# Row sums ordered by head, and two broadcast reads from DRAM where four stood, in a top-k attention and mixer kernel

## The chip, the core and the metric

The kernel runs on one core of one Trainium2 chip. The metric is the device time of one execution in microseconds (us); lower is better. A core has a matrix engine (PE, with its weight loads listed apart as PEld), a vector engine (DVE), an activation engine (ACT), a general engine (POOL), and a queue engine (SP) that here only issues transfers. Each engine takes its instructions strictly in the order of the program. Transfers (DMAs) are issued by SP and by ACT; on ACT an issue stands in the same order as its computing instructions.

## The reference

Attention over the 32 largest scores of each row, then a mixer with a low-rank token part and a two-layer channel part:

```python
# q, k, v: (8, 8, 576, 64)
scores = scale * np.matmul(q, k.transpose(0, 1, 3, 2))
kth = np.partition(scores, -32, axis=-1)[..., -32:-31]
scores = np.where(scores >= kth, scores, -1e9)
attn = np.exp(scores - np.max(scores, axis=-1, keepdims=True))
attn = attn / (np.sum(attn, axis=-1, keepdims=True) + 1e-09)
x = np.matmul(attn, v).transpose(0, 2, 1, 3).reshape(8, 576, 512)
# U: (576, 32), V: (32, 576), w_ch1: (512, 2048), w_ch2: (2048, 512)
u = x + (x.transpose(0, 2, 1) @ U @ V).transpose(0, 2, 1)
out = u + np.maximum(u @ w_ch1, 0.0) @ w_ch2
```

The division by the row sum is what the change touches: every row of `attn` has one sum, and the kernel multiplies by its inverse after the product with `v`.

## The kernel before, in words

The 64 heads are taken two at a time: 32 pairs `g`, four to a batch entry. The 576 rows of a head are four tiles of 128 (`t` 0 to 3) and a tail of 64 (`t` 4), in which the two heads of a pair share one tile. The program is one long hand-made order: a loop over steps, one tile each (the last tile of a pair and its tail share a step), and in each step a fixed sequence of calls for tiles in different stages. In the order in which a tile passes them:

- `scores` (L336, L381, L401): the score products on PE, copied to `Ssb` (the tail to `Stail`) by ACT.
- `fold`, `split` and `pair` (L432, L434, L435): each row is halved into its larger and smaller entries; POOL adds, DVE takes the maximum, POOL subtracts.
- `front` (L487, L485, L502, L515, L520): DVE finds the 32 largest of a row by rounds of "eight largest" and "replace them". ACT makes the negated row maximum (`nmax`, L506) and the threshold (`least`, L546), masks (L549; POOL subtracts in L550), and takes exponentials (L439), whose sums over the row go to one column of a small tile `den` each. `den` has nine columns: two heads by four tiles, and the tail.
- `blocks` and `back` (L576, L582, L591): DVE transposes the exponentials in blocks, four DMAs from SP put them into a DRAM tile `away`, and one DMA from ACT reads it back as `PT`. `back` runs one step after `blocks`.
- `values` (L688, L691, L700): the product with `v`, features on the partitions, copied to `XT` by ACT. It is not yet divided by the row sums.
- `inverse` (L629, L631, L635), for pairs 4 to 31: once a pair's nine sums are there, DVE inverts and transposes them to nine rows of 128, and four DMAs from SP write these to a DRAM tile `rd` of nine rows: row `2t+h` for tile `t` and head `h`, and row 8 for the tail, with 64 numbers for each head.
- `scale` (L641 to L651), two thirds of a step later: DMAs from ACT read `rd` into a tile of 128 by 576, `sc`, so that each of the 64 partitions of a head holds all inverse sums of that head.
- `mixed` (L719, L720, then L725 to L778): POOL multiplies `XT` by `sc` into `uT`; then comes the token part of the mixer. L777 uses the tile `sc` again as a scratch.
- `mlp` (L810, L823, L828, L839, L840): the channel part of an earlier batch entry. Its products are spread between the others by `fill()`; ACT applies the rectifier (`hT`, L823) and copies (`oT`, L839), POOL adds `uT` (L840).

For the first four pairs the sums are used in another layout (`den4`), without `rd` and `sc`. The attention of all pairs with the channel part of earlier entries between it lasts to about 1545 us; after it the channel part of the last entry runs alone (`closing`).

Two things set when a DMA can start. It stands in its engine's order. And in the built program every DMA of SP and ACT, in the order of the program, is given one of eight semaphores in turn; before it is issued, its engine waits until the last DMA with the same semaphore has landed, unless an earlier wait already made that sure. So a DMA can hold its engine back for the sake of a transfer that it has nothing else to do with.

Of the kernel before, what the change touches and what calls it, by code (L numbers as in the profile page):

```python
# [26 lines left out]
def kernel(  # L27
# [28 lines left out]
    nc = tc.nc  # L56
    B, H, S, D = q.shape
    P = 128
# [4 lines left out]
    NT, TAIL = 4, 64  # L63
    MAIN = NT * P
    HALF = S // 2
    assert S == MAIN + TAIL and D == 64 and H % 2 == 0 and C == 512 and TOPK % 8 == 0
    NPAIR = H // 2
# [69 lines left out]
    def half(h):  # L137
        return slice(h * D, (h + 1) * D)
# [298 lines left out]
    def weigh(chunk, E, nmax, total=None):  # L437

        nc.scalar.activation(E, chunk, AF.Exp, bias=nmax, scale=SCALE, accum_out=total)  # L439

    def ways(g, t):

        if (g, t) == (NPAIR - 1, NT - 1):
            return (0,), (), (1,)
        if (g, t) == (NPAIR - 1, NT):
            return (0,), (), ()
        if t == NT:
            return (), (), (0,)
        return ((), (1,), (0,)) if g < NPAIR else ((), (), (1, 0))
# [4 lines left out]
    def front(tiles):  # L454

        lanes = []
        for g, t in tiles:  # L460
            if t == 0:
                dens[g] = small.tile([P, 2 * NT + 1], F32, tag="den", name="den", bufs=3)
            S2, den = S2s.pop((g, t)), dens[g]
            early, pooled, gaps = ways(g, t)
            n = S2.shape[1]
            fold_of = folds.pop((g, t), None)
            for c in (1, 0) if n == 2 else (0,):
                slot = c if n == 2 or len(tiles) == 1 else 2
                lanes.append((
                    slot,  # L470
                    S2[:, c],
                    den[:, 2 * t + c : 2 * t + c + 1],
                    [a[:, c] for a in fold_of] if fold_of else None,
                    "early" if c in early else "pooled" if c in pooled else "gap" if c in gaps else "",
                ))
        W = len(lanes)
        first = small.tile([P, 3, 8], F32, tag="first", name="first", bufs=3)
        nmax = small.tile([P, 3], F32, tag="nmax", name="nmax", bufs=4)
        curs, places, ms = {}, {}, {}
        halves = [(lane[0], *lane[3]) for lane in lanes if lane[3]]  # L480
        for at_, step in ((0, 0), (0, 1), (8, 0)):
            for slot, upper, lower in halves:
                spot = upper[:, HALF + at_ : HALF + at_ + 8]
                if step:
                    nc.vector.match_replace(lower, spot, lower, NEG)  # L485
                else:
                    nc.vector.max(spot, lower)  # L487
        for slot, chunk, _, fold_of, _ in lanes:
            if fold_of:
                curs[slot] = fold_of[0]  # L490
            else:
                curs[slot] = chunk
                if slot == 2:
                    places[slot] = attn.tile([P, S], F32, tag="tplace", name="place", bufs=1)
                else:
                    places[slot] = attn.tile(
                        [P, 2, HALF + TOPK // 2], F32, tag="upper", name="upper"
                    ).rearrange("p c n -> p (c n)")[:, 0:S]
            ms[slot] = first[:, slot]
        order = [lane[0] for lane in lanes]  # L500
        for c in order:
            nc.vector.max(ms[c], curs[c])  # L502
        yield
        for i in range(1, TOPK // 8):
            if i == 1:
                nc.scalar.mul(nmax[:, 0:W], first[:, 0:W, 0], -SCALE)  # L506
                Es = {}
                for c, chunk, _, _, way in lanes:
                    if way == "early":
                        Es[c] = attn.tile([P, S], F32, tag="E", name="E")  # L510
                        weigh(chunk, Es[c], nmax[:, c : c + 1])
            for c in order:

                nxt = places.pop(c, curs[c])
                nc.vector.match_replace(nxt, ms[c], curs[c], NEG)  # L515
                curs[c] = nxt
            m8 = small.tile([P, 3, 8], F32, tag="m8", name="m8", bufs=4)
            for c in order:
                ms[c] = m8[:, c]
                nc.vector.max(ms[c], curs[c])  # L520
            yield
        for c, chunk, total, _, way in lanes:
            if way == "pooled":
                gap = attn.tile([P, S], F32, tag="E", name="E")
                nc.gpsimd.tensor_scalar(gap, chunk, ms[c][:, 7:8], NEG, ALU.is_lt, ALU.mult)
                nc.gpsimd.tensor_tensor(chunk, chunk, gap, ALU.add)  # L526
        for c, chunk, total, _, way in lanes:
            if way == "early":
                nc.vector.scalar_tensor_tensor(
                    out=chunk,  # L530
                    in0=chunk,
                    scalar=ms[c][:, 7:8],
                    in1=Es[c],
                    op0=ALU.is_ge,
                    op1=ALU.mult,
                    accum_out=total,
                )
        if t == NT:
            del qkTs[g]
        yield  # L540
        gaps = [lane for lane in lanes if lane[4] == "gap"]
        if gaps:
            slots = [lane[0] for lane in gaps]
            lo, hi = min(slots), max(slots) + 1
            least = small.tile([P, 3], F32, tag="least", name="least", bufs=3)
            nc.scalar.mul(least[:, lo:hi], m8[:, lo:hi, 7], WIDEN)  # L546
            for c, chunk, *_ in gaps:
                gap = attn.tile([P, S], F32, tag="E", name="E")
                nc.scalar.activation(gap, chunk, AF.Relu, bias=least[:, c : c + 1], scale=-WIDEN)  # L549
                nc.gpsimd.tensor_tensor(chunk, chunk, gap, ALU.subtract)  # L550
            yield
        rest = [lane for lane in lanes if lane[4] != "early"]
        if len(gaps) > 1:
            c, chunk, total, *_ = rest.pop(0)
            weigh(chunk, chunk, nmax[:, c : c + 1], total)
            yield
        for c, chunk, total, *_ in rest:
            weigh(chunk, chunk, nmax[:, c : c + 1], total)
        if t == NT and g != NPAIR - 1:
            nc.scalar.activation(den, den, AF.Identity, bias=eps)  # L560
        yield
# [77 lines left out]
    def scale(g):  # L639

        rd = scales.pop(g)  # L641
        sc = attn.tile([P, S], F32, tag="scale", name="scale", bufs=1)
        scales[g] = sc
        for h in range(2):
            nc.scalar.dma_start(
                sc[half(h), 0:MAIN].rearrange("p (t n) -> p t n", t=NT),
                rd[0 : 2 * NT].rearrange("(t h) n -> h t n", h=2)[h : h + 1].to_broadcast([D, NT, P]),
            )
            nc.scalar.dma_start(
                sc[half(h), MAIN:S], rd[2 * NT : 2 * NT + 1, half(h)].to_broadcast([D, TAIL])  # L650
            )  # L651

    def values(g, t):

# [521 lines left out]
    t = 0  # L1176
# [5 lines left out]
    for n in range(STEPS + 2):  # L1182
        if n < STEPS:
            g, t = steps[n][0]
            if t == 0 and g < NPAIR:
                load(g + 1)
            if t == (1 if g < NPAIR else 2) and g + 1 < NP:
                ready = prep(g + 1)
            fronts[n] = front(steps[n])
            next(fronts[n])  # L1190
        else:
            t = NT
# [93 lines left out]
        if n < STEPS and n - 2 >= ALONE and len(tiles(n - 2)) > 1:  # L1286
            scale(steps[n - 2][0][0])
# [3 lines left out]
        if n >= STEPS:  # L1291
            if n == STEPS:
                inverse(NP - 1, 0, 2 * NT + 1)
                scale(NP - 1)
            weighted(n - 2)
# [61 lines left out]
```

## Time and profile before

| what | value |
| --- | --- |
| time, median of three runs | 1684.32 us (1682.92 to 1688.65) |
| the profiled execution | 1686.09 us, of which 1684.0 us are its span |
| mean granted PE clock | 0.963 |
| DMA packets | 295631, 189.42 MB; queue of SP 259728 packets, queue of ACT 35744 |
| `scale` reads of ACT | 56 of 128 KB (L645) and 56 of 16 KB (L649), two of each per pair for 28 pairs |
| `rd` writes of SP (L635) | 112 of 1.1 KB, median issue 316 ns |
| `PT` reads of ACT (L591) | 104 of 576 KB, median issue 326 ns |
| L719, multiply by `sc` | 56 on POOL, median 738 ns; L720 28, median 330 ns |

The span runs from the first to the last instruction of the program; the profiled execution's own time is 2.1 us longer. Busy time counts an engine's computing instructions; an engine that waits before a DMA issue counts as idle, and such issues are listed with a "q" behind the engine's name (ACTq, SPq). A number in square brackets behind an instruction is the idle time just before it and what ended that.

### The profile page before, as it was taken

The numbers are of one execution on the slowest core, as the hardware profiler recorded it, in microseconds if no ns is written. First come the engines' busy times: TensorE is split into PE (matmuls) and PEld (weight loads), VectorE is DVE, ScalarE is ACT, GpSimd is POOL, SyncE is SP. The second block draws the span as 40 slices with busy tenths as digits, with TensorE's granted clock in tenths as the row PEclk, the third lists the DMA queues.
The fourth block names the chain that finished last, engine by engine and source line by source line (L and its number), as shares of the span: only waits on it lengthen the run. The fifth ranks groups of instructions, "written<-read, shape, count | busy, mean of one in ns | idle before, by whom it ended". The sixth has DMA issues, their size and how long they took to land.

```text
span 1684.0 us, 30301 instructions
## 1 busy us (share of the span) xinstructions
PE 1569.8 (93%) x9638; PEld 1189.6 (71%) x9638; DVE 1546.0 (92%) x4393; ACT 992.5 (59%) x2475; POOL 1000.3 (59%) x853
## 2 busy tenths in 40 slices
PE   4667798999899999999999999999999999999999
PEld 2444466777577886778777787778777787778776
DVE  7999998899999999999999999999999999995452
ACT  4888777665655656556655566556655566564320
POOL 4778668666656565655656565655656565653620
PEclk7787798999999999999999999999999999999999
DMA  3323232254555555555455555554555555543001
GB/s 87 96 74 96 61 94 73 56 128 130 136 128 131 134 151 131 127 138 131 124 128 139 127 139 135 132 139 124 133 128 132 133 140 136 132 126 109 10 1 29
DMA packets 295631, 189.42 MB, mean 112 GB/s; under 512 B 178768, under 2 KB 279984, under 8 KB 295472
## 3 DMA queue, kind: packets, MB, share of 16 engines
q1 hardware_dynamic: 259728, 117.62, 30.2%
q10 hardware_dynamic: 35744, 69.88, 13.6%
q8 instruction: 76, 1.25, 0.3%
q14 instruction: 83, 0.68, 0.1%
HBM read 116.49 MB, written 70.91 MB: 111 GB/s over the span
## 4 chain that ended last, share of the span: by engine, by line
DVE 47%; PE 33%; DMA 8%; SPq 4%; issue 3%; ACT 2%; POOL 1%; ACTq 0%; DVEq 0%; POOLq 0%
DVE m L520 13%; DVE upper L515 11%; PE mm L828 9%; PE mm L810 8%; DVE y L576 5%; DVE first L502 4%; DVE upper L487 4%; DMA ld<-in_k_dram 3%; PE sc L336 3%; DVE place L515 3%; PE mm L904 3%; DVE lower L485 3%; PE O L691 2%; DMA PT<-away 2%; PE sc L904 2%
## 5 line engine op out<-in xcount | busy, mean ns | idle before, releaser
L810 PE MATMUL mm<-uT,w 128*128 128x320 f32 (+1 forms) x1792 | 468.1, 413 | 14.5 <-ACT hT L823 14.1
L550 POOL TENSOR_TENSOR Ssb<-Ssb,E 128x576 f32<-128x576 f32 x243 | 340.0, 1419 | 208.8 <-ACT E L549 208.4
L828 PE MATMUL mm<-hT,w 128*128 128x320 f32 (+1 forms) x1792 | 462.8, 408 | 0.0
L810 PEld LDWEIGHTS mm<-uT,w 128*128 128x128 f32 x1792 | 336.1, 192 | 120.2 <-ACT hT L823 23.3
L828 PEld LDWEIGHTS mm<-hT,w 128*128 128x128 f32 x1792 | 332.5, 190 | 93.6 <-issue 11.0
L520 DVE MAX8 m<-upper 128x8 f32<-128x304 f32 (+1 forms) x780 | 377.8, 539 | 0.7
L515 DVE MATCH_REPLACE8 upper<-m,upper 128x304 f32<-128x304 f32 (+1 forms) x520 | 266.8, 534 | 0.0
L435 POOL TENSOR_TENSOR lower<-lower,upper 128x576 uint32<-128x576 uint32 x108 | 152.9, 1416 | 162.0 <-DVE upper L434 161.7
L439 ACT ACTIVATE Ssb<-Ssb,nmax 128x576 f32<-128x576 f32 x258 | 201.8, 783 | 32.9 <-POOL Ssb L526 9.9
L432 POOL TENSOR_TENSOR lower<-Ssb 128x576 uint32<-128x576 uint32 x108 | 152.4, 1411 | 93.3 <-ACT Ssb L381 48.7
L487 DVE MAX8 upper<-lower 128x8 f32<-128x288 f32 x432 | 176.8, 461 | 15.9 <-POOL lower L435 15.8
L336 PE MATMUL sc<-qkT 64*128 64x288 f32 (+1 forms) x1056 | 179.6, 462 | 11.0 <-ACT Ssb L390 7.8
L549 ACT ACTIVATE E<-Ssb,least 128x576 f32<-128x576 f32 x243 | 176.3, 769 | 4.2
L381 ACT COPY Ssb<-sc 128x576 f32<-128x576 f32 x216 | 127.8, 644 | 61.6 <-PE sc L336 61.6
L576 DVE STREAM_TRANSPOSE y<-Ssb 128x512 f32<-128x512 f32 (+1 forms) x312 | 157.7, 581 | 0.3 <-ACT Ssb L439 0.2
L823 ACT ACTIVATE hT<-mm 128x320 f32<-128x320 f32 (+1 forms) x224 | 91.3, 410 | 102.7 <-PE mm L810 97.9
L691 PE MATMUL O<-PT,va 128*64 128x128 f32 x2048 | 144.5, 285 | 0.0
L336 PEld LDWEIGHTS sc<-qkT 64*128 64x128 f32 (+1 forms) x1056 | 96.0, 197 | 52.0 <-issue 17.4
L691 PEld LDWEIGHTS O<-PT,va 128*64 128x64 f32 x2048 | 113.3, 140 | 16.4 <-issue 2.0
L515 DVE MATCH_REPLACE8 upper<-first,upper 128x304 f32<-128x304 f32 x216 | 100.4, 487 | 0.0
L485 DVE MATCH_REPLACE8 lower<-upper,lower 128x288 f32<-128x288 f32 x216 | 96.3, 465 | 0.0
L434 DVE TENSOR_TENSOR upper<-sc,Ssb 128x576 f32<-128x576 f32 x108 | 83.3, 772 | 11.5 <-ACT Stail L401 11.5
(264 smaller groups left out, 2246.9 us busy)
## 6 DMA issues: line engine op xcount, KB each, us to landing
away<-y SPq DMA_DIRECT2D x416, 144.0 KB
PT<-away ACTq DMA_DIRECT2D x104, 576.0 KB
raw<-in_moe_w_ch_dram SPq DMA_DIRECT2D x32, 512.0 KB
va<-in_v_dram SPq DMA_DIRECT2D x64, 128.0 KB
out_dram<-ob SPq DMA_DIRECT2D x59, 128.0 KB
scale<-rd ACTq DMA_DIRECT2D x56, 128.0 KB
ld<-in_q_dram SPq DMA_DIRECT2D x108, 64.0 KB
ld<-in_k_dram SPq DMA_DIRECT2D x108, 64.0 KB
```

Of the source, the lines that this page charges most:

```text
L336: nc.tensor.matmul(out, lhsT=qkT[half(h), 0, cols(t)], rhs=qkT[half(h), 1, lo:hi], start=True, stop=True,)
L435: nc.gpsimd.tensor_tensor(bottom, bottom, top.bitcast(U32), ALU.subtract)
L439: nc.scalar.activation(E, chunk, AF.Exp, bias=nmax, scale=SCALE, accum_out=total)
L487: nc.vector.max(spot, lower)
L515: nc.vector.match_replace(nxt, ms[c], curs[c], NEG)
L520: nc.vector.max(ms[c], curs[c])
L549: nc.scalar.activation(gap, chunk, AF.Relu, bias=least[:, c : c + 1], scale=-WIDEN)
L550: nc.gpsimd.tensor_tensor(chunk, chunk, gap, ALU.subtract)
L576: nc.vector.transpose(y[:, :, i * NT : i * NT + c].rearrange("p r c j -> p c r j"), E2[:, a : a + c * P].rearrange("p (c r j) -> p c r j", ...
L691: nc.tensor.matmul(O[half(h)], lhsT=va[:, h, j, :], rhs=PT[:, NT * h + j], start=False, stop=(j == NT - 1),)
L810: nc.tensor.matmul(ph[:, 0:w], lhsT=first_layer(cc, f), rhs=uT[:, cc, lo:hi], start=(cc == 0), stop=(cc == NC - 1),)
L828: nc.tensor.matmul(po[:, 0:w], lhsT=w2[:, f, c * P : (c + 1) * P], rhs=hTs[f][:, 0:w], start=(f == 0), stop=(f == NF - 1),)
```

## The change

The sums of pairs 4 to 31 get another column of `den`: `4h+t` where `2t+h` stood. `rd` then has the four rows of a head next to each other, which is 512 numbers in one piece. `scale` reads all 128 partitions with one DMA for the four tiles and one for the tail, where it had two of each, one per head. The source of the first is two pieces of 512, each repeated 64 times (2 x 64 x 512), its target 128 partitions of 512. The source of the second is 2 x 64 x 64.

```diff
@@ front
             for c in (1, 0) if n == 2 else (0,):
                 slot = c if n == 2 or len(tiles) == 1 else 2
+                spot = NT * c + t if g >= NPAIR and t < NT else 2 * t + c
                 lanes.append((
                     slot,
                     S2[:, c],
-                    den[:, 2 * t + c : 2 * t + c + 1],
+                    den[:, spot : spot + 1],
@@ scale
         sc = attn.tile([P, S], F32, tag="scale", name="scale", bufs=1)
         scales[g] = sc
-        for h in range(2):
-            nc.scalar.dma_start(
-                sc[half(h), 0:MAIN].rearrange("p (t n) -> p t n", t=NT),
-                rd[0 : 2 * NT].rearrange("(t h) n -> h t n", h=2)[h : h + 1].to_broadcast([D, NT, P]),
-            )
-            nc.scalar.dma_start(
-                sc[half(h), MAIN:S], rd[2 * NT : 2 * NT + 1, half(h)].to_broadcast([D, TAIL])
-            )
+        full = rd[0 : 2 * NT].rearrange("(h t) n -> h () (t n)", h=2)
+        nc.scalar.dma_start(sc[:, 0:MAIN], full.to_broadcast([2, D, MAIN]))
+        ends = rd[2 * NT : 2 * NT + 1].rearrange("o (h n) -> (o h) () n", h=2)
+        nc.scalar.dma_start(sc[:, MAIN:S], ends.to_broadcast([2, D, TAIL]))
```

## The prediction, written before the changed kernel was run

> **What bounds the kernel now.** I read the busy table first, then the sums from 290 to 1540 us, the stretch in which `scale` runs 27 of its 28 times, then the waits, the `scale` tile, and last the chain and the timeline around single pairs. The busy table:
>
> ```profile
> PE 1569.8 (93%) x9638; PEld 1189.6 (71%) x9638; DVE 1546.0 (92%) x4393; ACT 992.5 (59%) x2475; POOL 1000.3 (59%) x853
> ```
>
> PE and DVE are both nearly full. The sums of that stretch (us, then busy time of PE, PEld, DVE, ACT, POOL, then clock, DMA share, GB/s) say it sharper:
>
> ```profile
> 290.00:1540.00 1250.00, 1225.49 (x7780) 940.03 (x7775) 1219.09 (x3700) 742.66 (x1877) 753.47 (x636) 0.99 0.52 129
> ```
>
> DVE idles 30.9 us of 1250 and PE 24.5 us. The change leaves the work of both as it is, so it can save no more than about 25 us here, however much it takes off ACT. Who makes them wait:
>
> ```profile
> DVE upper L487 <- POOL lower L435: 15.8, 9, 3.5
> ...
> PE mm L810 <- ACT hT L823: 14.1, 14, 2.8
> ...
> DVE upper L434 <- ACT Stail L401: 11.5, 6, 3.5
> ```
>
> All three have ACT behind them somewhere. The tile `scale` shows what ACT's queue pays (minimum, median and maximum ns of an issue):
>
> ```profile
> L645 ACTq DMA_DIRECT2D scale<-rd x56: 592/622/863, 271.5 to 1544.8; - x56
> L649 ACTq DMA_DIRECT2D scale<-rd x56: 469/626/1035, 272.2 to 1545.5; - x56
> ```
>
> The timeline of ACT at one pair shows more than the issues' own time:
>
> ```profile
> 934.68 0.62 ACTq L645 DMA_DIRECT2D scale<-rd  x1
> 935.14 0.19 ACT L439 ACTIVATION_READ_ACCUMULATOR Ssb<-Ssb,nmax 128x1 f32 x1
> 935.34 0.63 ACTq L649 DMA_DIRECT2D scale<-rd  x1
> 935.99 0.62 ACTq L645 DMA_DIRECT2D scale<-rd  x1
> 939.07 0.47 ACTq L649 DMA_DIRECT2D scale<-rd  x1
> 939.59 0.20 ACT L506 ACTIVATE nmax<-first 128x2 f32<-128x2 f32 x1 [4.26 <-DMA ld<-in_k_dram]
> 939.70 0.64 ACT L823 ACTIVATE hT<-mm 128x256 f32<-128x256 f32 x2
> ```
>
> The fourth read starts 2.5 us after the third ended: its semaphore was last given to a load of `k`, and ACT stands until that has landed. The `hT` that PE wants is behind it, and then the scores, and then DVE:
>
> ```profile
> 940.12 4.51 PE L810 MATMUL mm<-uT,w 128*128 128x256 f32 x12 [2.83 <-ACT hT L823]
> ```
>
> ```profile
> 950.00 0.76 DVE L434 TENSOR_TENSOR upper<-sc,Ssb 128x576 f32<-128x576 f32 x1 [3.48 <-ACT Stail L401]
> ```
>
> Every fourth pair is hit otherwise: ACT's `oT` is late, so POOL's L840, so L435 behind it, so DVE:
>
> ```profile
> 798.57 0.72 POOL L840 TENSOR_TENSOR oT<-oT,uT 128x256 f32<-128x256 f32 x1 [5.68 <-ACT oT L839]
> ```
>
> ```profile
> 800.71 0.82 DVE L487 MAX8 upper<-lower 128x8 f32<-128x288 f32 x2 [2.35 <-POOL lower L435]
> ```
>
> **What the change takes away.** From the first `scale` issue of a pair to the end of the fourth ACT's queue spends 104.8 us over 28 pairs (added up from the timeline); 33.6 us of it are waits before the fourth, in 22 pairs. In the changed program two reads are left, 2 x 0.63 = 1.3 us a pair or 36 us, and 2 of 28 second reads still wait for a foreign DMA. So ACT gets back 69 us. ACT is busy 59% and most of that is worth nothing; what counts is the idle time of PE and DVE that traces to it:
> - 3 to 5.5 us after a pair's first read PE waits for `hT` at 561, 750, 940, 1132 and 1320 us (0.44, 1.00, 2.83, 1.78, 2.08), and 11 to 15.5 us after it DVE waits in L434 (1.00, 0.84, 3.48, 1.25, 2.76). Both engines lose the same time, so I count the smaller of each pair: 7.4 us. The upper bound is DVE's 9.3.
> - 6 to 8 us after the first read DVE waits in L487 at 611, 801, 993, 1181 and 1370 us (2.04, 2.35, 2.33, 0.73, 0.69, together 8.1). PE has only 0.75, 0.50, 0.45, 0 and 0 us idle in those pairs' 48 us. What DVE wins it would lose again at the next scores. I take PE's 1.7; the bounds are 0 and 8.1.
>
> Gain: 7.4 + 1.7 = 9.1 us, bounds 7.4 and 17.4.
>
> **What it adds.** The moved bytes stay 288 KB a pair, but the first dimension of the source is now 2. The trace holds one row that bears on this: the `rd` writes have 9 rows. Among the packet records of SP's queue those of 4 bytes, one for each engine that ends its share of a DMA, are 20672; 1341 DMAs on 16 engines would make 21456, and 112 x (16 - 9) = 784 are missing exactly. ACT's 218 DMAs, all with a first dimension of 64 or 128, make 218 x 16 = 3488. So the number of engines follows the first dimension, and with 2 rows against 128 partitions I take two engines, 64 packets of 2 KB each. No row has such a packet here. By the medians of read packets (46 ns for 1 KB, 159 ns for 4 KB) it takes 84 ns; by the time in which a `PT` read delivers its 8 packets of 4.6 KB per engine (2.47 us median), 137 ns. I take 84, nearest in size. The first packet comes 2.4 us after the first issue (median now, behind a `PT` read); 64 x 0.084 = 5.4 gives +7.8. From +5.5 on, the four `away` writes share the engine (32 packets of 84 ns, 2.7 us), up to half of the time: +9.7. With 137 ns it is +11.2, and +13.9 with sharing. The tail read follows, 64 x 18 ns = 1.2 us: about +10.9. Now the last of the four lands 4.2 to 6.6 us after the first issue.
>
> Here the Trainium skill speaks against the change. Its page "DMA: Bandwidth & Descriptors", section "Rules for kernel authors", says that an outermost dimension below 16, a broadcast's for one, confines the whole DMA to that many engines, and its section on why a semaphore goes up by 16 adds that the count must divide the outer dimensions of both sides. The nine rows on nine engines agree with it. By the rule the read lands at about +9.7; with sixteen engines it would land at about +3.1, and the time would be the first rival's.
>
> Who waits for the later landing:
> - POOL's L719 needs the first read, 10.4 to 16.4 us after the first issue now (27 pairs; the last pair 8.6). At +9.7 it waits for nothing; L720 comes 1.4 us later, after +10.9. If this cover goes, L435 behind it is late, and DVE's L487 after that: at 955 us there is 0.9 us between them.
> - SP. In eleven pairs the fourth `away` write gets a semaphore of the first read: it goes at +9.7 where it goes at +6.4 to +9.0 now, and behind it loads of `k` with many us to spare. It lands 2.1 us after its issue (2.11 in the chain at 849.35), so at +11.8, while ACT's L591 wants that tile at +10.0 to +15.4 in these pairs: pair by pair 5 us of new waiting. Loads in the other pairs are held 2 to 3 us; they are for the next pair, some 20 us later.
> - ACT. In eight pairs the `PT` read of L591 waits for the tail read itself: +10.9 against +8.7 to +10.2, together 10 us.
>
> That is 5 + 10 = 15 us of new waiting on ACT, at another place of its order. The 33.6 us of waiting that go cost DVE 17.4 us of idle, 0.52 for each; at that price 15 us cost 8 us. The waits of ACT for `away` now (9.5, 5.3 and 2.9 us before three of its lines) stand before no visible wait of PE for `hT`, which speaks for 0. I take 3, nearer to these, since it is the same wait. At the end of the run ACT is free 1.4 us sooner and the last `sc` lands up to 2 us later than its use at +8.6: 0, bounds -1.4 and +2. The reordered columns of `den` cost nothing: same instructions, another address.
>
> **Sum.** -9.1 + 3 + 0 = -6.1 us on the span of 1684.0; the profiled execution with its 1686.09 lies in the upper part of the three runs, so I set the sum against their median: 1684.3 - 6.1 = 1678. Own range of this case: 1684.3 - 17.4 = 1667 to 1684.3 - 7.4 + 8 = 1685.
>
> **Rivals.**
> - Sixteen engines after all. For it: all other reads of ACT use sixteen; against it: the nine rows. Then `sc` is there early and nothing new waits: 1684.3 - 9.1 = 1675. Chance 0.08.
> - The wait only moves: ACT's stand before L591 costs PE as much as that before the fourth read. For it: the slack there is small (at 851.99 L591 issues 0.5 us after `away` landed). Against: `hT` is not just behind it. 9.1 given back: 1684. Chance 0.09.
> - Slower: the two engines are too slow for L719. Place: POOL, from L719 by L435 to DVE's L487, in some 24 pairs whose use lies between +10.4 and +12.5. It decides from a first landing of about +12 on. At 137 ns with sharing, +13.9, against a use of +11.5 and 0.9 us of slack: late by 1.5 us; I put 1.2 since some pairs have more slack. 24 x 1.2 = 29 us, less the gain of 9.1: +20, 1704. For it: DMA engines are half busy and PE and DVE have no reserve, so any new wait shows at once. Against: 84 ns. Chance 0.36.
>
> **How the numbers follow.** The forecast has 0.47. I call a difference of over 0.3% (5 us) told from none. Faster: 0.36 of the forecast, since 1678 is close to the bound of 1679.3, and 0.07 of the first rival: 0.43. Same: 0.11 + 0.01 + 0.07 = 0.19. Slower: 0.02 of the second, 0.36 of the third: 0.38. The range reaches from 1665, a little past the largest gain, to 1706, past the middle of the slow case.
>
> **What would show it.** Of each step: two `scale` issues and no stand of 2 us before the second; ACT's queue with about 23300 packets if two engines are used (112 completions, not 896); no wait in L434 at the fourth pairs; L487 waits smaller; L719 not waiting for a DMA. It is wrong if L719, or PE's L688 through a late `PT`, waits in most pairs, or if the idle time of DVE stays at 31 us though ACT is free.

## The result, and the profile after

| | before | after |
| --- | --- | --- |
| median time, six runs each | 1686.51 us (1682.92 to 1689.25) | 1698.90 us (1696.91 to 1701.88) |
| ratio, with its 95% interval | | 1.0075 (1.0057 to 1.0092) |
| profiled execution, its span | 1686.09, 1684.0 | 1698.27, 1696.4 |

The changed kernel is slower by 0.75%. What was to go is gone, and something the prediction held for harmless has come. The busy table and the sums of the stretch from 290 to 1540 us of the changed kernel (us, busy time of PE, PEld, DVE, ACT, POOL, then clock, DMA share, GB/s):

```profile
PE 1569.5 (93%) x9638; PEld 1187.0 (70%) x9638; DVE 1549.5 (91%) x4393; ACT 994.2 (59%) x2475; POOL 1000.5 (59%) x853
```

```profile
290.00:1540.00 1250.00, 1216.62 (x7723) 930.26 (x7724) 1217.13 (x3690) 738.25 (x1864) 747.31 (x631) 0.99 0.50 128
```

DVE now idles 1250 - 1217.1 = 32.9 us there, where it was 30.9, and PE 33.4, where it was 24.5. DVE's total is nearly the same, but its causes are others. The tile `scale` first (minimum, median and maximum ns of an issue):

```profile
L646 ACTq DMA_DIRECT2D scale<-rd x28: 508/513/1086, 270.5 to 1550.7; - x28
L648 ACTq DMA_DIRECT2D scale<-rd x28: 516/517/781, 271.6 to 1551.3; - x28
```

ACT at one pair (start, duration, what):

```profile
747.72 0.51 ACTq L646 DMA_DIRECT2D scale<-rd  x1
748.27 0.52 ACTq L648 DMA_DIRECT2D scale<-rd  x1
748.83 0.20 ACT L507 ACTIVATE nmax<-first 128x2 f32<-128x2 f32 x1 [0.18 <-DVE upper L434]
748.94 0.37 ACT L820 ACTIVATE hT<-mm 128x256 f32<-128x256 f32 x1
```

The second read follows the first at once, and `hT` starts 0.15 us after its end: ACT has its queue back. The groups of DVE whose waits were to go (busy time, mean ns, idle time before them):

```profile
L488 DVE MAX8 upper<-lower 128x8 f32<-128x288 f32 x432 | 172.0, 439 | 3.0 <-POOL lower L435 3.0
...
L434 DVE TENSOR_TENSOR upper<-sc,Ssb 128x576 f32<-128x576 f32 x108 | 79.9, 740 | 2.1 <-ACT Stail L401 2.1
```

These were 15.8 (then L487) and 11.5 us: 22.2 us of DVE's waiting are gone. Now the waits (us in all, times, longest):

```profile
DVE qkT L306 <- DMA ld<-in_k_dram: 29.1, 17, 2.9
...
PE O L685 <- DMA PT<-away: 15.9, 16, 2.2
...
PE mm L807 <- ACT hT L820: 10.3, 12, 1.5
```

The first line did not stand in the profile before at all. L306 is the transpose of `q` and `k` of a coming pair on DVE; it waits 17 times for the loads of `k`. The second line was smaller before:

```profile
PE O L688 <- DMA PT<-away: 5.1, 6, 1.6
```

What SP itself waits for ahead of its issues explains the first:

```profile
SPq L258 <- DMA scale<-rd: 26.0, 17, 3.8
SPq L583 <- DMA ld<-in_k_dram: 23.8, 15, 3.2
...
SPq L263 <- DMA scale<-rd: 14.0, 13, 1.8
...
SPq L583 <- DMA scale<-rd: 13.2, 9, 4.0
```

L258 and L263 are the loads of `q` and `k`, L583 the `away` writes. None of them uses `sc`. They wait for its reads only because they are given the same semaphore, 26.0 + 14.0 + 13.2 = 53.2 us in 39 waits; before it was 2.7 us in one. The chain of waits around one pair shows the whole path (start, duration, what):

```profile
748.27 10.82 DMA scale<-rd
759.09 0.02 issue
759.11 0.60 SPq L258
...
760.42 0.59 SPq L258
761.01 0.04 issue
761.05 3.62 DMA ld<-in_k_dram
...
764.86 1.38 DVE qkT L306
```

A read of `sc` takes 10.8 us to land; until then SP stands before four loads of `k`; the last of them, issued at 761.05, takes 3.6 us; DVE waits for it. Over 25 pairs, by medians from the first `scale` issue: the last load of `k` was issued at +9.5 and landed at +11.1, and L306 began at +15.4. Now it is issued at +12.3 and lands at +15.8, and L306 begins at +16.7. The load lost 2.8 us to SP's stand and 1.9 us to a slower landing, 4.7 in all.

Between the first and the last pair's `scale` the changed kernel takes 8.3 us longer (1550.70 - 270.49 against 1543.50 - 271.54), and from the last one to the end 5.2 us longer (145.7 against 140.5). The start is 1.1 us shorter. Together that is the 12.4 us of the spans.

### The profile page after: what moved, and what is told of

The parts are those of the page before. It is cut to its first block, busy times and chain, and to the rows that moved or that the text cites. A ratio compares the mean times of both kernels' runs of the same rounds, so it can differ in the third digit from the quotient of the medians.

```text
span 1696.4 us, 30175 instructions
## 1 busy us (share of the span) xinstructions
PE 1569.5 (93%) x9638; PEld 1187.0 (70%) x9638; DVE 1549.5 (91%) x4393; ACT 994.2 (59%) x2475; POOL 1000.5 (59%) x853
## 3 DMA queue, kind: packets, MB, share of 16 engines
q10 hardware_dynamic: 23312, 69.87, 12.7%
## 4 chain that ended last, share of the span: by engine, by line
DVE 53%; DMA 24%; PE 11%; SPq 6%; issue 2%; ACT 1%; ACTq 1%; POOL 1%; DVEq 0%; POOLq 0%
DVE m L521 14%; DVE upper L516 12%; DMA scale<-rd 12%; DMA ld<-in_k_dram 5%; DVE y L577 5%; DVE upper L488 5%; DVE first L503 5%; DVE place L516 3%; DVE lower L486 3%; DMA ld<-in_q_dram 3%; PE mm L901 3%; SPq L258 2%; PE mm L825 2%; DVE qkT L306 2%; DMA away<-y 2%
## 5 line engine op out<-in xcount | busy, mean ns | idle before, releaser
L807 PE MATMUL mm<-uT,w 128*128 128x320 f32 (+1 forms) x1792 | 464.3, 410 | 12.9 <-ACT hT L820 10.3
L825 PEld LDWEIGHTS mm<-hT,w 128*128 128x128 f32 x1792 | 333.0, 191 | 93.7 <-issue 10.3
L521 DVE MAX8 m<-upper 128x8 f32<-128x304 f32 (+1 forms) x780 | 367.0, 511 | 0.7
L435 POOL TENSOR_TENSOR lower<-lower,upper 128x576 uint32<-128x576 uint32 x108 | 152.9, 1416 | 196.8 <-DVE upper L434 196.5
L516 DVE MATCH_REPLACE8 upper<-m,upper 128x304 f32<-128x304 f32 (+1 forms) x520 | 259.7, 507 | 0.0
L488 DVE MAX8 upper<-lower 128x8 f32<-128x288 f32 x432 | 172.0, 439 | 3.0 <-POOL lower L435 3.0
L577 DVE STREAM_TRANSPOSE y<-Ssb 128x512 f32<-128x512 f32 (+1 forms) x312 | 154.2, 545 | 0.5 <-ACT Ssb L439 0.2
L547 ACT ACTIVATE least<-m 128x2 f32<-128x2 f32 (+2 forms) x131 | 26.7, 204 | 127.8 <-DVE m L521 127.7
```

What stands on the lines that cost most here:

```text
L435: nc.gpsimd.tensor_tensor(bottom, bottom, top.bitcast(U32), ALU.subtract)
L577: nc.vector.transpose(y[:, :, i * NT : i * NT + c].rearrange("p r c j -> p c r j"), E2[:, a : a + c * P].rearrange("p (c r j) -> p c r j", ...
L807: nc.tensor.matmul(ph[:, 0:w], lhsT=first_layer(cc, f), rhs=uT[:, cc, lo:hi], start=(cc == 0), stop=(cc == NC - 1),)
L825: nc.tensor.matmul(po[:, 0:w], lhsT=w2[:, f, c * P : (c + 1) * P], rhs=hTs[f][:, 0:w], start=(f == 0), stop=(f == NF - 1),)
```

## The experiments

Edits are shown against the changed kernel, unless said otherwise. Times are medians; each ratio is to runs of the kernel before on the same chip. "Landing" is the median time from a pair's first `scale` issue to the end of its last `scale` packet: 5.55 us before, 10.86 after.

### The order of the sums alone, and reads on sixteen engines

The first kernel keeps the new order of `den` and `rd`, and reads each head by itself again, 64 copies of one row:

```diff
-full = rd[0 : 2 * NT].rearrange("(h t) n -> h () (t n)", h=2)
-nc.scalar.dma_start(sc[:, 0:MAIN], full.to_broadcast([2, D, MAIN]))
-ends = ...
+full = rd[0 : 2 * NT].rearrange("(h t) n -> h (t n)", h=2)
+for h in range(2):
+    nc.scalar.dma_start(sc[half(h), 0:MAIN], full[h : h + 1].to_broadcast([D, MAIN]))
+    nc.scalar.dma_start(sc[half(h), MAIN:S], rd[2 * NT : 2 * NT + 1, half(h)].to_broadcast([D, TAIL]))
```

> Columns of den as in the changed kernel, but four reads again, one pair per head: 64 copies of 512 contiguous numbers, and 64 copies of 64. First dimension of the source 64. My theory (the two-row source puts the read on two engines, it lands near +11 us, SP is held at the semaphore it shares with that read, the second half of the k loads is late, DVE waits in L306): ACT's queue has 18 packets-worth of completions more again, 16 for each of 112 reads; last landing at +4 to +6.6 us as before; DVE's wait in L306 under 1 us in total; time that of before within 0.3% (1681 to 1691). Rival (the reordered sums, or the longer packets of 2 KB, cost the time): as slow as the changed kernel, about 1699.

Measured: 1684.44 us, ratio 1.0012 (0.9995 to 1.0028); landing 5.48. The new order and the packets of 2 KB cost nothing and bring nothing.

The second has two reads, but one per head, each of 576 numbers in one piece. For that the tail's row lies between the heads in `rd`, `sc` is 640 wide, and the multiplication of the tail is two instructions of 64 partitions:

```diff
-spot = NT * c + t if g >= NPAIR and t < NT else 2 * t + c
+spot = 2 * t + c if g < NPAIR else NT if t == NT else (NT + 1) * c + t
...
+full = rd.rearrange("r n -> (r n)").rearrange("(h n) -> h n", h=2)
+for h in range(2):
+    at_ = 0 if h else TAIL
+    nc.scalar.dma_start(sc[half(h), at_ : at_ + S], full[h : h + 1].to_broadcast([D, S]))
```

> Two reads as in the changed kernel and at the same places of the program, but one per head: the rows of rd are ordered so that a head's five pieces are 576 contiguous numbers, read in 64 copies into a sc of 640 columns (main part at 64 to 575); the tail's multiplication on POOL becomes two instructions of 64 partitions. My theory: sixteen engines, landing by about +4 us, no hold of SP, DVE's L306 wait gone, and the gain that was expected (the waits in L434 and L487, 9 to 17 us) is there: 1670 to 1678. Rival (two DMAs fewer shift the round of the eight semaphores, and that is what holds SP, whatever the landing): the L306 wait of 29 us stays, about 1699. Rival (ACT's release brings nothing, PE is full): 1684.

Measured: 1664.78 us, ratio 0.9887 (0.9867 to 0.9907), landing 4.6. L306 waits for nothing and SP never for a `scale` read. So two reads are 1.1% faster than four, as long as they are on sixteen engines. From the first pair's first `scale` issue to the last pair's, a stretch with the same work in both kernels, first the kernel before and then this one (columns as above):

```profile
271.54:1543.50 1271.96, 1245.55 (x7930) 954.97 (x7928) 1234.45 (x3742) 760.28 (x1919) 769.67 (x650) 0.99 0.51 128
```

```profile
271.05:1521.71 1250.66, 1235.03 (x7930) 951.97 (x7928) 1235.84 (x3745) 763.40 (x1919) 779.01 (x678) 1.00 0.52 131
```

The stretch is 21.3 us shorter. DVE is busy as long as before, and its idle time falls by 22.7 us, from 37.5 to 14.8. PE has the same 7930 matmuls. Its idle time falls by 10.8 us, from 26.4 to 15.6, and the other 10.5 us come out of what the profile counts as busy. Half of these lie in the 896 products of L810 with 256 columns (L815 here): 387 ns each before and 381 now. The same number of columns in the products of L828, which wait for nothing, takes 381 ns in both. So part of PE's busy time before was not needed for this work.

### Another order on SP

If the stand of SP only matters to the loads of `k`, issuing them ahead of the `scale` reads should cure it:

```diff
+            next(coming, None)
             scale(steps[n - 2][0][0])
...
-            next(coming, None)
+            if n - 2 < ALONE or len(tiles(n - 2)) == 1:
+                next(coming, None)
```

> The changed kernel with its two-engine reads, but in the program order the second half of the next pair's k loads is put ahead of them (and so ahead of the away writes of that step in SP's order). The read is as slow as in the changed kernel (landing near +11). My theory (SP is held in front of the k loads): the L306 wait of 29 us falls under 3 us and the time to 1672 to 1684; what is left over e2 is the held away writes and PT reads. Rival (the two hot engines slow everything that passes them, no matter who is issued when): 1693 or more, and the waits show at PT or k loads all the same.

Measured: 1710.98 us, ratio 1.0168 (1.0142 to 1.0195): slower still, and a miss. L306 waits no more, but SP's stand has moved to the next issues behind, the `away` writes (SP's waits, then those of the other engines):

```profile
SPq L583 <- DMA scale<-rd: 55.1, 36, 3.9
```

```profile
ACT Ssb L439 <- DMA away<-y: 31.5, 10, 5.4
...
ACT hT L820 <- DMA away<-y: 22.2, 8, 6.4
DVE y L577 <- DMA away<-y: 19.1, 17, 4.0
```

These writes are wanted sooner than `k`: ACT stands before the `PT` read for them with `hT` behind it, and DVE may not overwrite `y`. The stand was not removed, only given to a more urgent transfer.

The same order with the second kernel's two reads:

> e2 and the earlier k loads of e3 together. My theory: as e2 within 0.3%, since nothing holds the k loads there; if the away writes now stand behind the loads in SP's order and come late, it is up to 0.5% slower than e2.

Measured: 1666.10 us, ratio 0.9894 (0.9875 to 0.9914), the same as without it. The order itself costs nothing where there is no stand.

### The number of engines, and nothing else

Both kernels are the second one with the 64 copies written as 2 x 32 and as 4 x 16. Bytes, packets of data, DMAs and semaphores stay:

```diff
-full = rd.rearrange("r n -> (r n)").rearrange("(h n) -> h n", h=2)
+full = rd.rearrange("r n -> (r n)").rearrange("(h n) -> h () n", h=2)
...
-full[h : h + 1].to_broadcast([D, S])
+full[h : h + 1].to_broadcast([2, D // 2, S])
```

(with `[4, D // 4, S]` in the other).

> e2 with one thing changed: the 64 copies of a source are written as 2 x 32 (the first dimension is 2, nothing else differs: the same bytes, the same 128 packets of 2304 bytes, the same two DMAs at the same places of the program, the same order of all engines). If the number of engines is the cause, it goes the way of the changed kernel: last landing near +10 us, L306 waiting for k loads, 1692 to 1700. If the cause is in the order of the sums, in the tail's columns or in anything else that e2 has otherwise than the changed kernel, it stays at e2's 1665.

> As before, with 4 x 16 copies: four engines, 32 packets each at some 95 ns, landing near +6 us, which is before SP wants the semaphores (+6.4 to +9 in the kernel before). If SP's hold is the cause, there is a threshold and this is as fast as e2, 1664 to 1670. If the price is the load on single engines, it lies between, at about 1680.

ACT's queue in the second kernel, with two and with four (packets, MB, share):

```profile
q10 hardware_dynamic: 20512, 69.87, 13.4%
```

```profile
q10 hardware_dynamic: 19728, 69.87, 12.4%
```

```profile
q10 hardware_dynamic: 19840, 69.87, 12.7%
```

On this queue a DMA leaves one packet of 4 bytes for each engine it uses. 56 x (16 - 2) = 784 are missing in the one and 56 x (16 - 4) = 672 in the other, exactly. The Trainium skill, "DMA: Bandwidth & Descriptors", section "Rules for kernel authors", says that an outermost dimension under 16 confines a DMA to at most so many engines, and these counts agree with it. Its row on transfers to partition halves in the same section advises one transfer of 128 partitions in their place, because both halves use all sixteen engines anyway. Here the merged transfer falls to two engines, so the advice does not carry over: the changed kernel, which merges the halves, takes 1698.90 us, and two halves on sixteen engines take 1664.78. No run has a merged transfer on sixteen engines.

Measured with two engines: 1696.32 us, 1.0058 (1.0038 to 1.0079), landing 10.05, and the wait is back:

```profile
DVE qkT L306 <- DMA ld<-in_k_dram: 24.2, 13, 3.2
```

With four: 1671.02 us, 0.9914 (0.9897 to 0.9931), landing 6.8, one wait of L306 of 0.7 us, 3.0 us of SP's waiting on `scale`. So the number of engines makes 1.0058 - 0.9887 = 1.7% by itself, 29 us: all that the changed kernel lost, and the gain with it.

### The load on two engines without SP's stand at it

Two engines can hurt in two ways: SP stands until the late read lands, or other transfers that need the two engines come late. Here the second kernel gets a read that nobody uses, 128 rows of 2 KB into a free tile, in 25 of 28 pairs; POOL issues it, and POOL's DMAs have semaphores of their own, so SP does not wait for it. The first dimension of its source is two in the one kernel, shown here, and 128 copies of one row in the other:

```diff
+spread = ...
+two = rows_[0 : 2 * MAIN].rearrange("(h n) -> h () n", h=2)
+nc.gpsimd.dma_start(spread, two.to_broadcast([2, D, MAIN]))
```

> e2, and beside each pair's reads (25 of 28 pairs) POOL issues one more read of 128 packets of 2 KB from a source of two rows into a tile that nobody reads. POOL's DMAs have semaphores of their own, so two engines get the load that the changed kernel gives them, and SP is not held by it. If SP's hold is the whole price, the time is that of the next kernel within 0.5%. If the load on two engines is the price, it is slower than the next by 1% or more and k loads or PT reads are late.

> The same with a source of 128 copies, on sixteen engines: the price of a DMA issued by POOL alone. POOL has 40% idle time, but the issue stands in its order ahead of work that DVE waits for: 1665 to 1690, by what an issue costs.

Measured: 1678.51 us, 0.9961 (0.9946 to 0.9976), on two engines and 1668.35, 0.9896 (0.9876 to 0.9916), on sixteen. The extra read is on few engines as meant: its last packet lands 10.3 us after the pair's first `scale` issue, against 5.3 on sixteen, and two to four of its packets are under way at once, as with the changed kernel's reads (three or four), against ten to eighteen. Two things are not as in the changed kernel. The trace does not tell which engines POOL's read uses, so they need not be the two of ACT's reads. And POOL's read goes in 64 packets of 4 KB, and with two rows it leaves 448 packets of 8 bytes more each time, which the one on sixteen engines does not have.

With these limits, the load on two engines is worth 10.2 us. PE waits 15.8 us for `PT` with it and 7.4 without, L306 4.8 us for `k` against none. Part of that is again SP standing, at transfers that land late; three of its waits in the kernel with two engines:

```profile
SPq L258 <- DMA out_dram<-ob: 22.3, 15, 2.8
...
SPq L263 <- DMA away<-y: 12.2, 12, 2.3
...
SPq L583 <- DMA ld<-in_k_dram: 10.0, 5, 4.0
```

On sixteen engines the first two do not occur, and the third is 4.2 us.

A short transfer on two engines is another matter. This kernel has three reads, the main part by head on sixteen engines as in the first kernel and the tail in one read of two rows as in the changed one:

> Three reads: the main part one per head (64 copies of 512, sixteen engines), the tail one read of 2 x 64 copies on two engines (64 packets of 256 bytes each, some 1.2 us). What counts is not that two engines are used but for how long: landing near +5, no hold of SP on it, no L306 wait. ACT's third issue and its semaphore cost something: between e2 and before, 1668 to 1678. If a two-row source is slow by its form, whatever its size: 1685 or more.

Measured: 1666.32 us, 0.9900 (0.9872 to 0.9927), landing 5.1. The 64 packets of 256 bytes on two engines do no harm that these runs can tell. And three reads bring nearly what two do: the gain comes with dropping the fourth read, which takes ACT's stand with it. The third read costs nothing that can be told, though ACT's queue spends 49.0 us on three reads and 32.4 on two.

### SP's stand without the load

The other half: the second kernel with loads of 32 bytes that nobody uses, issued by SP once a pair ahead of the last four loads of `k`. They hold SP and load almost nothing. There are eight or sixteen, so that every other DMA keeps its semaphore:

```diff
+def hold(count):
+    for i in range(count):
+        nc.sync.dma_start(idle[:, i], q[0, 0, i : i + 1, 0:8])
...
+            if n - 2 >= ALONE and len(tiles(n - 2)) > 1:
+                hold(8)
             next(coming, None)
```

In the control the eight stand behind `next(coming, None)`.

> The kernel with two reads on sixteen engines, plus eight loads of 32 bytes that nobody uses, issued by SP once a pair just ahead of the second half of the loads of k. Eight keeps every DMA's semaphore what it was. They hold SP some 2.5 us (each waits for the last DMA with its semaphore, the four away writes among them) and put almost nothing on the DMA engines. Theory A, the hold alone does it: the last load of k is issued at about +12.5 us after the first scale read, as in the changed kernel (+12.9), where it was +9.8; it lands in 2 us and not in 2.8, so L306 waits in some pairs only: 1668 to 1676, and 3 to 10 us over the control with the eight loads behind the loads of k. Theory B, it is the load on two engines: no difference from the control, and both at 1664 to 1670.

> The control: the same eight loads of 32 bytes, issued just behind the loads of k. SP has some 5 us to spare there. Both theories: 1664 to 1670, L306 not waiting. If it is slower than that, the small loads cost something besides the hold, and the other two kernels are to be read against this one.

> Sixteen loads of 32 bytes ahead of the loads of k: a hold of some 5 us, so that k's last load is issued at about +15 and lands at about +17, where L306 wants it at +15.1. Theory A: L306 waits some 1.5 to 2 us in most of 26 pairs, 25 to 50 us of DVE's idle time, and the kernel takes 1685 to 1710 us, with sixteen engines in every scale read. Theory B: within 5 us of the control.

| | last load of `k` issued at | L306 waits for `k` | time | ratio |
| --- | --- | --- | --- | --- |
| eight behind (control) | +8.8 us | 0 | 1666.71 us | 0.9889 (0.9862 to 0.9916) |
| eight ahead | +13.6 | 17.7 us, 18 times | 1685.84 | 1.0012 (0.9998 to 1.0027) |
| sixteen ahead | +17.0 | 111.5 us, 25 times | 1776.25 | 1.0544 (1.0520 to 1.0569) |

SP at one pair with eight ahead:

```profile
753.64 1.98 SPq L588 DMA_DIRECT2D away<-y  x4
755.67 2.73 SPq L131 DMA_DIRECT2D idle<-in_q_dram  x8
758.44 0.59 SPq L263 DMA_DIRECT2D ld<-in_k_dram  x1
759.07 0.63 SPq L268 DMA_DIRECT2D ld<-in_k_dram  x1
759.75 0.58 SPq L263 DMA_DIRECT2D ld<-in_k_dram  x1
760.38 0.63 SPq L268 DMA_DIRECT2D ld<-in_k_dram  x1
```

And L306 (L311 here) with eight, then with sixteen:

```profile
DVE qkT L311 <- DMA ld<-in_k_dram: 17.7, 18, 2.3
```

```profile
DVE qkT L311 <- DMA ld<-in_k_dram: 111.5, 25, 6.3
```

With every `scale` read on sixteen engines, a delay on SP alone costs 19 us over the control, and all that two reads had gained; 17.7 us of DVE's waiting for `k` stand against it. Both slow ones came out above what was expected, since the hold is longer than the 2.5 and 5 us assumed: 4.8 and 8.2 us by the table. Past the end of the slack the time grew about as fast as the delay: from eight to sixteen the loads go 3.4 us later, times 26 pairs is 88 us, and the time grew by 90.4. (The granted clock from 290 to 1540 us was 0.97 with sixteen and 1.00 in the control; what that adds was not separated.) The slack in the control is about 4: L306 begins at +14.8, and in the two held kernels it begins 1.7 and 2.1 us (medians) after the last issue, so 14.8 - 8.8 - 2 = 4.0.

## Why the prediction went wrong

The time lay in the range, but the direction was wrong: the forecast was 6 us less, and it became 12 us more. That it lay in the range is luck: the upper part of the range was there for a wait of POOL's L719 that did not come. One of the prediction's own signs of being wrong did come: DVE's idle time stayed at 32.9 us though ACT was free. Step by step:

- **ACT gets back its queue: right.** Two issues follow each other without a stand, 0.51 and 0.52 us each where 0.63 was assumed.
- **Two engines: right, to the packet.** Predicted about 23300 packets on ACT's queue; 23312 were there. A packet of 2 KB takes 84 ns, as taken. The last packet lands at +10.86, where +10.9 was worked out, but that close only because two misses cancel: the first read lands at +8.8 and not at +9.7, and the tail takes 2.1 us more and not 1.2. (The prediction's own terms, half of the engine from +5.5 on, would give +10.1 and not +9.7.)
- **L719 waits for nothing: right.** The multiplication (now L716) never waits for a DMA. With it the slower rival falls as it was put: its sign was right; its place, POOL's L719 by L435 to DVE, was not. Sixteen engines, the first rival, did not come.
- **"Loads in the other pairs are held 2 to 3 us; they are for the next pair, some 20 us later": this is the step that failed.** The hold was right, 2.8 us at the median. The 20 us were not read from the trace. In the trace of before, the last load of `k` lands at +11.1 and L306 starts at +15.4, in the same pair's stretch. That is 4.3 us, of which 0.9 pass between the last packet and L306 when it does wait (+15.8 and +16.7 after). Some 3.4 us of slack stood against 4.7 us of delay: 29.1 us of waiting on DVE, put at nothing. Where the stand of SP alone delayed these loads by 4.8 us, the same wait came to 17.7 us.
- **The landing of other transfers was left out of that step.** The loads of `k` land 2.8 us after their issue, not 1.6. The prediction shared the two engines between `scale` and `away`, but asked only how late `scale` would be, not how late the others.
- **New waits on ACT, 15 us, priced at 3:** the 15 were nearly right. ACT's waits for `away` grew from 17.7 to 27.4 us, and 4.2 us for `scale` came. The price was not measured by itself; PE's wait for `PT` grew from 5.1 to 15.9 us. The second rival, which put the price there, had a true part, but the larger loss was on SP.
- **The gain of 9.1 us was mis-sized.** With sixteen engines the reads bring 1.0% to 1.1%, 17 to 19 us of 1684. The working took the smaller idle time of PE and DVE in each pair, since PE had none to give. The second kernel shows that PE had: about half of what it gave came out of time that the profile counts as busy. DVE's side of the sum, 17.4 us, named as the upper bound, was about the size. The first bound of the prediction, the 24.5 us of PE's idle time in the whole stretch, was not passed.
- **The end of the run, taken at 0 with bounds -1.4 and +2, was +5.2 us.** While the last `scale` read is landing, the last `away` writes land late too: 7.4 us after SP's first issue of them, where it was 4.4. The `PT` read behind them is issued 7.1 us after the pair's first `scale` issue, where it was 4.4, and its last packet lands at +11.1, where it was +7.7. That is 3.5 of the 5.2 us. PE waits for it (after, then before):

```profile
1562.45 0.46 PE L685 MATMUL O<-PT,vd 128*128 128x128 f32 x2 [2.22 <-DMA PT<-away]
```

```profile
1551.63 0.46 PE L688 MATMUL O<-PT,vd 128*128 128x128 f32 x2 [0.23 <-DMA PT<-away]
```

In one sum: -19 us for two reads fewer (the second kernel against before), +29 us for two engines in place of sixteen, gives +10; 12.4 were measured.

**What is open.** SP's stand alone is shown to be enough for a loss of 19 us, and a load on few engines, with SP's stands that it brings, for 10. The two were measured with other delays than the changed kernel has, and do not simply add up; how its own loss divides between them was not tried. Nor was it separated which part of the gain belongs to ACT's stand and which to the two issues that it no longer makes.

**The better version.** Two reads on sixteen engines, 1664.78 us, are 1.1% faster than the kernel before and 1.9% by the ratios (0.9887 over 1.0075) than the changed one.

## What to carry to other kernels

When transfers are merged, look at what the merged source has as its first dimension: a first dimension of two puts the transfer on two engines, and two transfers with 64 rows each can be the better choice. For a transfer that lands later, list what its issuing queues have behind each wait on its semaphore, and take the slack of each from the trace, from its landing to its first use in the same pair, never from the plan of the program. PE's busy time in the profile is no fixed sum: here it fell by 10.5 us for the same matmuls once the waits went. So do not cut an estimate down to PE's idle time around single waits; look at the other full engine, here DVE, as well.

## What the runs showed of the hardware that was not expected

- The issue of a `scale` read on ACT took 513 and 517 ns (medians) for those of two rows, where those of 64 rows took 622 and 626 ns before. That the shape alone decides is not shown: the 64-row reads of the second kernel took 558 ns, and the same reads 612 in the control with eight loads behind.
- The same 128 packets of 2.3 KB land later on fewer engines, but not in proportion: at 4.6 us on sixteen, 6.8 on four, 10.05 on two. Four cost 0.3% (0.9914 against 0.9887, and the intervals overlap), two 1.7%; L306 waits often in the last of these only.
- The busy time that the profile gives for a matmul is not fixed: 387 ns in the kernel before and 381 in the second kernel for the same 896 products of L810, 381 in both for those of L828.
